# Random-feature attention and a Mish feed-forward on one core: query and key units shifted by one step, and Mish of chunk 0 given priority

## The chip, the cores and the metric

The kernel runs on one core of one Trainium2 chip. The time is device microseconds of one execution; several executions are made and their median is given. A profile shows one more execution, instruction by instruction.

## What is computed

Attention with random features over 8 batches, 8 heads, 576 rows, 64 elements a head and 128 features, and a feed-forward on the result (512 to 2048 to 512), which has Mish between its two products:

```python
def phi(x):
    proj = einsum('bhsd,md->bhsm', x, omega)
    h = proj - sum(x * x, -1) / 2
    h = h - max(h, -1)
    return exp(h) / sqrt(m)
kv  = einsum('bhsm,bhsd->bhmd', phi(k_s), v);  z = sum(phi(k_s), 2)
num = einsum('bhsm,bhmd->bhsd', phi(q_s), kv)
den = einsum('bhsm,bhm->bhs', phi(q_s), z) + 1e-06
x   = (num / den)            # 4608 rows of 512
h   = x @ w_in               # 512 -> 2048
g   = h * tanh(softplus(h))  # Mish
out = g @ w_out              # 2048 -> 512
```

## The kernel before

**Tiles.** Queries come as 36 tiles q0 to q35 of 128 rows with all heads, keys as 4 units per batch (k0_0 is batch 0, heads 0 and 1). The feed-forward goes by chunks of 256 rows: chunk 0 to 3 alone (`ff_in(c)`, `ff_out(c)`), the rest in pairs (`pair_in`, `pair_out`). Most products are made of three fp16 products of high and low parts. At the start, before the weights are split into these parts, the fp32 values are multiplied directly: batches 0 and 1 of the keys (KF = 2), query tiles 0 to 4 (QF = 5) and chunk 0.

**A unit.** `features` (L348) loads a tile, for fp16 units splits it (`in_parts`, L339: a cast on ScalarE and a residual on POOL), projects it on TensorE into PSUM (tiles pk, pq), takes the maximum on VectorE (mxk, mxq) and the exponential on ScalarE (ek, eq). A key unit is then multiplied with the values (pkv, L455 and L490). A query tile below QF goes on in `q_first` (L574): eight transposes on TensorE (pt, L581) with two copies by ScalarE (qp), the product with kv (pn, L592), then on VectorE the denominator (rd, L596) and x (L605), whose copy, residual and transposing DMA into xT are in `x_parts` (L563). Later tiles are transposed by a DMA (L525) and multiplied at L540, with x at L556.

**Weights.** Eight blocks of each matrix come as 64-bit words. `w_task` (L187) assembles fp32 from them (Prelu on ScalarE L198, POOL L201, VectorE L207) and takes the maximum (wmax, L213). `scale_w` makes one scale (s_w) of the eight maxima; `w_split` (L228) then casts a block on ScalarE and makes the residual on VectorE (L82).

**Chunk 0.** `ff_in(0)` (L692) makes 8 PSUM tiles ph, each copied by ScalarE into g with `later(1, cast, ...)`; at the last of them `later(2, mish0)` schedules Mish in place over both halves of g (gr = 1 first, then gr = 0). `ff_out0` (L797) goes over the blocks from f = 15 downward (po, L804).

**The order of the work.** The program is emitted in slots. A slot emits one piece of the feed-forward and then runs `step()`, which goes through an agenda of generators: `yield n` puts the rest of a generator n slots later. `FIRST` (L825) lists the slots at which the units are given in the order k0_0 to k0_3, q0 to q3, k1_0 to k1_3, q4 to q8, k2_0; `GAP` (L840) says how many slots pass between a unit's steps. `FF0` = 17 is the slot at which `ff_in(0)` starts, one ph every two slots; `ff_in(1)` starts at slot 33, `ff_out0` at 49, `ff_in(2)` at 65, alternating with `ff_out(1)`. The compiler then orders each engine's instructions: among those that it reckons ready, the one emitted first goes first. `tc.high_priority(PRIO)` with PRIO = 400 makes an instruction count as emitted 400 instructions earlier. On the chip each engine runs its list strictly in that order.

**PSUM.** ps_h and ps_o have two banks each (ph, po), ps_a four (pk, pq, pt, pn, pkv). A late key unit takes three of ps_a at once, a query tile's pn two.

Of the kernel before, what the change touches and what calls it, by code (L numbers as in the profile page):

```python
# [15 lines left out]
AF = mybir.ActivationFunctionType  # L16
# [14 lines left out]
def tile_kernel(  # L31
# [17 lines left out]
    FT = DF // P  # L49
    CH = 256  # L50
    NCH = NT * P // CH
    FG = 8
    FQ = 4
# [10 lines left out]
    act, dve, pool = nc.scalar, nc.vector, nc.gpsimd  # L64

    def cast(eng, out, in_, scale=1.0):

        if eng is act:
            return act.activation(out, in_, AF.Copy, scale=scale)  # L69
        elif isinstance(scale, float) and scale == 1.0:  # L70
            eng.tensor_copy(out, in_)  # L71
        else:
            eng.tensor_scalar_mul(out, in_, scale)
# [20 lines left out]
    def spin(n, left, right):  # L94
        pi = ps_o.tile([P, 512], F32, tag="o", name=f"spin{nc.next_id()}")
        for _ in range(n):
            nc.tensor.matmul(out=pi[:, 0:right.shape[1]], lhsT=left, rhs=right, start=True, stop=True)  # L97
# [143 lines left out]
    def wi(a, k, f):  # L241
        must(1, "s", 0, f * P * KT // BW)

        o = k * (BW // KT) + f * P % (BW // KT)
        return slots[f * P * KT // BW][:, a, o:o + P]
# [3 lines left out]
    def did(*key):  # L249
        done[key] = done.get(key, 0) + 1  # L250

    def must(n, *key):
        assert done.get(key, 0) >= n, key
# [24 lines left out]
    for i in range(2):  # L278
        t = const.tile([P, 2, 10, D1], F16, name=f"vb{i}")
# [221 lines left out]
    def spans(lo, n):  # L501

        res = []
        for b in range(lo // S, (lo + n - 1) // S + 1):
            res.append((b, max(lo, b * S) - lo, min(lo + n, (b + 1) * S) - lo))
        return res
# [56 lines left out]
    def x_parts(nth, t, x):  # L563
        xs = sb.tile([P, 2, H * D], F16, tag="xs", name=f"xs{t}", bufs=2)
        xf = x.rearrange("p h d -> p (h d)")
        cast(act if nth < 20 else by("x", nth), xs[:, 0], xf)
        rest(by("xlo", nth), xs[:, 1], xf, xs[:, 0])
        yield 1
        nc.sync.dma_start_transpose(
            out=x_at(t), in_=xs.rearrange("p a c -> p (a c)"),  # L570
        )
        did("x", t // 4)

    def q_first(nth, t, e, off):  # L574

        qp = sb.tile([P, H, P], F32, tag="ap", name=f"qp{t}", bufs=2)
        for g in range(2):
            hs = slice(4 * g, 4 * g + 4)
            pt = ps_a.tile([P, 4, P], F32, tag="a", name=f"pt{t}_{g}")
            for i in range(4):  # L580
                nc.tensor.transpose(out=pt[:, i, :], in_=e[:, 4 * g + i, :], identity=ident)  # L581
            cast(act, qp[:, hs, :], pt)
        yield 1
        x = sb.tile([P, H, D], F32, tag="x", name=f"x{t}", bufs=2)
        rd = sb.tile([P, H, 1], F32, tag="rd", name=f"rd{t}")
        for g in range(2):
            hs = slice(4 * g, 4 * g + 4)
            pn = ps_a.tile([P, 4, D1], F32, tag="a", name=f"pn{t}_{g}", padded_shape=[P, 4, P])
            for i in range(4):
                for b, lo, hi in spans(t * P, P):  # L590
                    must(HP, "kvf", b)
                    nc.tensor.matmul(  # L592
                        out=pn[lo:hi, i, :], lhsT=qp[:, 4 * g + i, lo:hi], rhs=kvf[b][:, 4 * g + i, :],
                        start=True, stop=True,
                    )
            dve.tensor_single_scalar(out=rd[:, hs], in_=pn[:, :, D:D1], scalar=EPS, op=ALU.add)  # L596
            dve.reciprocal(out=rd[:, hs], in_=rd[:, hs])
            if t * P < CH:
                xt = dve.tensor_tensor(
                    out=x[:, hs, :], in0=pn[:, :, 0:D], in1=rd[:, hs].broadcast_to([P, 4, D]),  # L600
                    op=ALU.mult,
                )
                continue
            for b, lo, hi in spans(t * P, P):
                xt = dve.scalar_tensor_tensor(  # L605
                    out=x[lo:hi, hs, :], in0=pn[lo:hi, :, 0:D], scalar=vstate[b][2][lo:hi],
                    in1=rd[lo:hi, hs].broadcast_to([hi - lo, 4, D]), op0=ALU.mult, op1=ALU.mult,
                )
        anchors[30 + t] = (xt.ins,)
        if t * P >= CH:  # L610
            yield from x_parts(nth, t, x)
            return
        yield 1
        px = ps_a.tile([P, KT, P], F32, tag="a", name=f"px{t}")
        for i in range(KT):
            nc.tensor.transpose(out=px[:, i, :], in_=x[:, 2 * i:2 * i + 2, :], identity=ident)
        anchors[40 + t] = (cast(act, xT0()[:, :, off:off + P], px).ins, xt.ins)
        if off == 0:
            spin(2, ident, x[:, 0:4, :].rearrange("p h d -> p (h d)"))
        did("x0")  # L620
# [4 lines left out]
    def xT0():  # L625
        return xT[0][:, 0:2 * KT * CH].bitcast(F32).rearrange("p (k s) -> p k s", k=KT)
# [10 lines left out]
    def g0(gr):  # L637
        return gT[0, gr].rearrange("p a f s -> p (a f s)").bitcast(F32).rearrange("p (f s) -> p f s", f=FG)
# [32 lines left out]
    def ff_in(c):  # L671

        must(4 if c > 2 else 2, "x", c // 2) if c else must(2, "x0")
        lo = CH * (c == 3)
        parts = (slice(0, P), slice(P, CH)), (slice(0, CH),)
        sp = [(b_scales(b) if c else None, lo, hi) for b, lo, hi in spans(c * CH, CH)]
        for gr in range(FT // FG):
            gT[c, gr] = sb.tile([P, 2, FG, CH], F16, tag="g", name=f"g{c}_{gr}", bufs=GB)
            for q in range(FG // FQ):
                if c:  # L680
                    h = sb.tile([P, FQ, CH], F32, tag="ht", name=f"h{c}_{gr}_{q}", bufs=HB)
                else:
                    h = g0(gr)[:, q * FQ:(q + 1) * FQ]
                for j in range(0, FQ, 2):
                    ph = ps_h.tile([P, 2, CH], F32, tag="h", name=f"ph{c}_{gr}_{q}_{j}")
                    for part, i in ((part, i) for part in parts[(c, gr, q, j) != (0, 0, 0, 0)] for i in range(2)):
                        f = gr * FG + q * FQ + j + i
                        mm = [(a, y, k) for a, y in ((1, 0), (0, 1), (0, 0)) for k in range(KT)]
                        if c == 0:
                            mm = [(None, None, k) for k in range(KT)]  # L690
                        for n, (a, y, k) in enumerate(mm):
                            ff_mm[0] = nc.tensor.matmul(  # L692
                                out=ph[:, i, part], lhsT=wi(a, k, f) if c else wi0(k, f),
                                rhs=x_two(c // 2)[:, y, k, lo:lo + CH] if c else xT0()[:, k, part],
                                start=n == 0, stop=n == len(mm) - 1,
                            )
                    if c == 0:

                        later(1, cast, act, h[:, j:j + 2, :], ph)
                        if gr == FT // FG - 1 and q == FG // FQ - 1 and j > 0:  # L700
                            later(2, mish0)
                    else:
                        later(1, mish, sp, h[:, j:j + 2, :], ph)
                        if j > 0:
                            later(2, g_split, c, gr, q, sp, h)
                    yield
# [49 lines left out]
    def mish(sp, h, ph):  # L756

        for us, lo, hi in sp:
            anchors["h"] = act.activation(h[:, :, lo:hi], ph[:, :, lo:hi], AF.Mish, scale=us[:, 0:1]).ins  # L759

    def mish0():
        for gr in reversed(range(FT // FG)):
            act.activation(g0(gr), g0(gr), AF.Mish)
            for q in range(FG // FQ):
                did("g", 0, q)

# [55 lines left out]
    GB, HB, QB = 4, 4, 1  # L822
    w_dma = nc.sync

    FIRST = (0, 1, 2, 3, 4, 4, 9, 9, 26, 28, 30, 32, 37, 40, 44, 58, 59, 63)  # L825
    WIS = (6, 7, 8, 9, 11, 12, 13, 14)
    W_MAX = (6, 5, 5, 4, 2, 2, 1, 1)
    WOS = (35, 34, 33, 32, 31, 30, 29, 28)
# [1 line left out]
    W_LOAD, W_LOAD1, W_GAP, PRIO = 1, 2, 1, 400  # L830
# [15 lines left out]
    def gap(what, name):  # L846
        if name in ("k0_0", "k0_1", "k0_2", "k0_3", "q0", "q1"):
            return GAP0[what]
        return GAP[what]

    def pace(c):
# [12 lines left out]
    def start(gen, after=0):  # L864
        agenda.append([slot[0] + after, gen])

    def later(after, fn, *args):
        def gen():
            fn(*args)
            yield 0  # L870
        start(gen(), after)
# [18 lines left out]
    for t in range(NT):  # L890
        last = (t * P + P - 1) // S
# [68 lines left out]
    start(v_task(0))  # L960
    for i, when in enumerate(FIRST):
        at(when, give)
# [94 lines left out]
```

## Time and profile before

| | |
|---|---|
| runs before | 938.16, 938.64, 938.83 us, median 938.64 |
| the profiled execution | 937.79 us, of which the profile's span is 936.0 us |
| granted TensorE clock | 1.00 |
| ScalarE, VectorE, POOL busy | 628.5 us, 529.6 us, 231.1 us |
| bytes moved by DMA | 82.05 MB, mean 88 GB/s |

Engines: PE is TensorE's matmuls, PEld its weight loads, DVE VectorE, ACT ScalarE, POOL GpSimd, SP the engine whose queue issues most DMAs. A row of the timeline has start, length, engine, line, operation, output and inputs with their shapes, and how many instructions it merges; in brackets stands how long the engine was idle before it and on whom it waited. A row of the waits has who waited, for whom, and us in total, times, longest. L69 and L78 to L82 are the helpers `cast` and `rest`, so there the tile's name tells what it is. ACT_TABLE_LOAD is the load of another set of functions into ScalarE.

### The profile page before, as it was taken

How to read it: one execution, taken by the hardware profiler on the slowest of the kernel's cores; microseconds unless marked ns; L12 is line 12 of the kernel's file. 1: busy time of each engine (PE TensorE's matmuls, PEld its weight loads, DVE VectorE, ACT ScalarE, POOL GpSimd, SP SyncE). 2: the span in 40 equal slices, each digit the busy share in tenths (PEclk: the TensorE clock that was granted, in tenths of full speed). 3: DMA queues.
4: the chain of work that ended last, by engine and by line, in shares of the span. 5: the costliest groups of instructions: out<-in, count | busy, mean ns of one | idle time of the engine just before them, and what ended most of it. 6: DMA issues, size and time to landing. Idle time of an engine off the chain costs nothing.

```text
span 936.0 us, 16681 instructions
## 1 busy us (share of the span) xinstructions
PE 921.6 (98%) x6797; PEld 532.4 (57%) x6797; DVE 529.6 (57%) x1019; ACT 628.5 (67%) x914; POOL 231.1 (25%) x143
## 2 busy tenths in 40 slices
PE   9998999999999999999999999999999999999998
PEld 6886866777655555555555555555555555444443
DVE  3899779855646784577357753784476345201200
ACT  5769998996949954897388747963887268304401
POOL 1331143541432233313232232323332121000000
PEclk9999999999999999999999999999999999999999
DMA  9975334623531256214531264203430242101001
GB/s 284 327 210 180 112 70 96 119 86 71 133 94 37 52 122 122 61 28 98 109 89 38 47 128 120 49 24 77 117 50 23 46 113 43 37 1 46 1 1 45
DMA packets 128204, 82.05 MB, mean 88 GB/s; under 512 B 106432, under 2 KB 106560, under 8 KB 128128
## 3 DMA queue, kind: packets, MB, share of 16 engines
q1 hardware_dynamic: 127392, 79.47, 34.1%
q10 hardware_dynamic: 736, 1.52, 0.6%
q8 instruction: 53, 0.87, 0.4%
q14 instruction: 23, 0.19, 0.1%
HBM read 46.37 MB, written 9.44 MB: 60 GB/s over the span
## 4 chain that ended last, share of the span: by engine, by line
PE 89%; DVE 5%; ACT 4%; issue 1%; DMA 0%; POOL 0%; ACTq 0%; DVEq 0%; POOLq 0%
PE po L745 31%; PE ph L721 31%; PE po L787 6%; PE ph L692 5%; PE pq L376 3%; PE pk L376 2%; PE pkv L490 2%; PE pn L540 2%; PE pkv L455 2%; PE po L804 1%; PE spin L97 1%; DVE wmax L213 1%; DVE w L207 1%; PE pk L391 1%; ACT ek L402 1%
## 5 line engine op out<-in xcount | busy, mean ns | idle before, releaser
L721 PE MATMUL ph<-xT,w 128*128 128x512 f16 x1344 | 298.4, 379 | 0.0
L745 PE MATMUL po<-wo,gp 128*128 128x512 f16 x1344 | 296.9, 379 | 0.0
L745 PEld LDWEIGHTS <-gp 128*128 128x128 f16 x1344 | 129.5, 98 | 149.9
L721 PEld LDWEIGHTS <-w 128*128 128x128 f16 x1344 | 129.1, 98 | 148.2
L82 DVE SCALAR_TENSOR_TENSOR gp<-h,us,gp 128x256 f16<-128x256 f32 (+6 forms) x104 | 103.7, 1013 | 121.9 <-ACT gp L69 121.6
L759 ACT ACTIVATE h<-ph,us 128x128 f32<-128x128 f32 (+6 forms) x240 | 108.0, 502 | 46.5 <-PE ph L721 42.4
L78 POOL TENSOR_TENSOR sq<-fq,sq 64x1024 f16<-64x1024 f32 x31 | 67.0, 2163 | 213.9 <-ACT sq L69 118.0
L692 PE MATMUL ph<-xT,w 128*128 128x256 f16 (+2 forms) x720 | 96.4, 290 | 1.3 <-DMA xT<-xs 0.8
L69 ACT ACTIVATE o<-po,us 128x512 f32<-128x512 f32 (+1 forms) x38 | 25.9, 682 | 98.9 <-PE po L745 92.5
L78 POOL TENSOR_TENSOR xs<-x,xs 128x512 f16<-128x512 f32 x34 | 46.0, 1353 | 157.0 <-issue 80.0
L78 POOL TENSOR_TENSOR sk<-fk,sk 64x1152 f16<-64x1152 f32 x24 | 58.3, 2431 | 90.2 <-ACT sk L69 90.1
L397 DVE TENSOR_REDUCE mxk<-pk 128x4 f32<-128x512 f32 (+1 forms) x96 | 49.9, 549 | 45.9 <-PE pk L376 33.4
L69 ACT ACTIVATE gp<-h,us 128x256 f16<-128x256 f32 (+6 forms) x104 | 73.8, 755 | 0.3
L397 DVE TENSOR_REDUCE mxq<-pq 128x4 f32<-128x512 f32 x72 | 46.6, 680 | 43.6 <-PE pq L376 39.5
L787 PE MATMUL po<-wo,g 128*128 128x512 f16 x288 | 65.4, 379 | 0.0
L78 DVE TENSOR_TENSOR qn<-eq,qn 128x1024 f16<-128x1024 f32 x31 | 39.1, 1262 | 43.0 <-ACT qn L69 43.0
L692 PEld LDWEIGHTS <-w 128*128 128x128 f16 x576 | 55.5, 98 | 10.9 <-issue 2.4
L759 ACT ACT_TABLE_LOAD x43 | 55.2, 1283 | 0.8
L69 ACT ACTIVATE sq<-fq 64x1024 f16<-64x1024 f32 x31 | 32.7, 1055 | 31.4 <-issue 29.9
L412 ACT ACT_TABLE_LOAD x39 | 50.0, 1283 | 0.7
L78 DVE TENSOR_TENSOR kp<-ek,kp 128x1152 f16<-128x1152 f32 x24 | 33.9, 1414 | 25.1 <-ACT kp L69 25.1
L78 POOL TENSOR_TENSOR vb<-vf,vb 128x640 f16<-128x640 f32 x24 | 35.9, 1499 | 46.3 <-DVE vb L71 34.5
(127 smaller groups left out, 1063.1 us busy)
## 6 DMA issues: line engine op xcount, KB each, us to landing
vf<-in_vL_dram SPq DMA_DIRECT2D x30, 325.0 KB, 3.2
out_dram<-o SPq DMA_DIRECT2D x36, 256.0 KB, 2.3
fq<-in_qT_dram SPq DMA_DIRECT2D x31, 256.0 KB, 3.4
fk<-in_kT_dram SPq DMA_DIRECT2D x24, 256.0 KB, 3.6
raw<-in_w_out_dram SPq DMA_DIRECT2D x5, 1024.0 KB, 7.1
wo<-in_w_in_dram SPq DMA_DIRECT2D x4, 1024.0 KB, 12.3
raw<-in_w_in_dram SPq DMA_DIRECT2D x4, 1024.0 KB, 14.6
wo<-in_w_out_dram SPq DMA_DIRECT2D x3, 1024.0 KB, 8.3
```

Source lines behind the costliest of these rows:

```text
L69: return act.activation(out, in_, AF.Copy, scale=scale)
L78: ins = eng.tensor_tensor(out=out, in0=in_, in1=hi, op=ALU.subtract)
L82: return eng.scalar_tensor_tensor(out=out, in0=in_, scalar=scale, in1=hi, op0=ALU.mult, op1=ALU.subtract)
L376: nc.tensor.matmul(out=pp[:, i, :], lhsT=left[:, o:o + P], rhs=right, start=j == 0, stop=j == len(terms) - 1,)
L397: sub = dve.tensor_reduce(out=mx[:, lo:hi], in_=pp[:, :m, :], axis=AX.X, op=ALU.max, negate=by_act)
L412: last = act.activation(e, e, AF.Exp, bias=lnt)
L455: nc.tensor.matmul(out=pkv[:, j, :], lhsT=e[:, t, :], rhs=vt[hp][:, u, :], start=i == 0, stop=i == 4,)
L692: ff_mm[0] = nc.tensor.matmul(out=ph[:, i, part], lhsT=wi(a, k, f) if c else wi0(k, f), rhs=x_two(c // 2)[:, y, k, lo:lo + CH] if c else x ...
L721: ff_mm[0] = nc.tensor.matmul(out=ph[:, 0, :], lhsT=wi(a, k, f), rhs=x[:, y, k, :], start=n == 0, stop=n == len(mm) - 1,)
L745: ff_mm[0] = nc.tensor.matmul(out=po[i], lhsT=gP[g, gr][:, a, f % FQ, i * P:(i + 1) * P], rhs=wo(y, f), start=f == 0 and (a, y) == parts[0 ...
L759: anchors["h"] = act.activation(h[:, :, lo:hi], ph[:, :, lo:hi], AF.Mish, scale=us[:, 0:1]).ins
L787: ff_mm[0] = nc.tensor.matmul(out=po[i], lhsT=gT[c, f // FG][:, a, f % FG, i * P:(i + 1) * P], rhs=wo(y, f), start=f == order[0] and (a, y ...
```

## The change

`q_first` gets a `yield 1` ahead of its transposes for t > 1. `FIRST`'s last entry, that of k2_0, goes from 63 to 64. The projection of q6 comes 3 instead of 2 slots behind its residual. The copies of chunk 0's last two ph tiles (gr = 1, q = 1) and all of `mish0` are emitted under `tc.high_priority(PRIO)`, and Mish of gr = 1 is made in two instructions, f = 12 to 15 first.

```diff
     def q_first(nth, t, e, off):
 
+        if t > 1:
+            yield 1
         qp = sb.tile([P, H, P], F32, tag="ap", name=f"qp{t}", bufs=2)
...
-                        later(1, cast, act, h[:, j:j + 2, :], ph)
+                        last = gr == FT // FG - 1 and q == FG // FQ - 1
+                        later(1, urgent if last else cast, act, h[:, j:j + 2, :], ph)
...
+    def urgent(*args):
+        with tc.high_priority(PRIO):
+            cast(*args)
+
     def mish0():
+        with tc.high_priority(PRIO):
+            mish0_()
+
+    def mish0_():
         for gr in reversed(range(FT // FG)):
-            act.activation(g0(gr), g0(gr), AF.Mish)
+            for q in ((1, 0) if gr else (slice(None),)):
+                w = g0(gr)[:, q * FQ:(q + 1) * FQ] if gr else g0(gr)
+                act.activation(w, w, AF.Mish)
             for q in range(FG // FQ):
                 did("g", 0, q)
...
-    FIRST = (0, 1, 2, 3, 4, 4, 9, 9, 26, 28, 30, 32, 37, 40, 44, 58, 59, 63)
+    FIRST = (0, 1, 2, 3, 4, 4, 9, 9, 26, 28, 30, 32, 37, 40, 44, 58, 59, 64)
...
     def gap(what, name):
         if name in ("k0_0", "k0_1", "k0_2", "k0_3", "q0", "q1"):
             return GAP0[what]
+        if what == "lo" and name == "q6":
+            return 3
         return GAP[what]
```

## The prediction

> **What bounds the kernel now.** I read the page's first two lines, the busy time by stages, TensorE's waits, and the chain of waits around the last of these that lies early.
>
> ```profile
> span 936.0 us, 16681 instructions
> PE 921.6 (98%) x6797; PEld 532.4 (57%) x6797; DVE 529.6 (57%) x1019; ACT 628.5 (67%) x914; POOL 231.1 (25%) x143
> ```
>
> TensorE is busy for 921.6 of 936.0 us, so no reordering can win more than the other 14.4 us. The stages (us in the stretch, then busy us of PE, PEld, DVE, ACT, POOL) say where these lie:
>
> ```profile
> 72.00:142.00 70.00, 65.48 (x504) 48.17 (x504) 55.70 (x98) 68.89 (x105) 17.38 (x10) 1.00 0.36 110
> 142.00:180.00 38.00, 35.57 (x316) 24.45 (x315) 32.78 (x73) 32.98 (x38) 16.78 (x9) 1.00 0.55 118
> 180.00:936.00 756.00, 752.12 (x5470) 402.39 (x5468) 388.83 (x735) 481.18 (x666) 176.69 (x99) 1.00 0.29 66
> ```
>
> From 180 us on TensorE idles for 3.88 us, and that is the tail behind its last matmul. All that the change can touch happens before 180 us. There two engines compete to be the bound: in 72 to 142 us ScalarE is busy for 68.89 of 70 us, more than TensorE with 65.48. The waits of TensorE (us in total, times, longest):
>
> ```profile
> PE po L804 <- ACT g L763: 1.8, 1, 1.8
> PE pk L376 <- DVE x L556: 1.6, 1, 1.6
> PE pq L376 <- POOL sq L78: 1.5, 1, 1.5
> PE pt L581 <- ACT eq L402: 1.3, 1, 1.3
> PE pk L391 <- ACT ek L402: 1.1, 1, 1.1
> PE ph L692 <- DMA xT<-xs: 0.8, 1, 0.8
> ```
>
> Four of these stand at places that the diff names: chunk 0's Mish (1.8), q6's projection (1.5), batch 2's keys (1.6), the transposes of q2 (1.3). Together 6.2 us. If each went and nothing took its place, the span would be 929.8 us. The sixth wait is why I don't believe that sum:
>
> ```profile
> 146.08 2.10 POOL xs L78
> 148.20 3.05 DMA xT<-xs
> 151.29 0.81 PE ph L692 x6
> ```
>
> Here TensorE has finished chunk 0's output and q7's projection, and the first matmul of ff_in(2) needs the transposed x of q5, which lands at 151.25. TensorE is 0.8 us early. If it gains 1.8 and 1.5 us before that point, it is 4.1 us early, and the transfer lands when it did. So what is won before 151 us counts only as far as this chain moves too, and the chain comes through the stretch in which ScalarE is full.
>
> **Part by part.** *Mish and the last cast.* ScalarE and, as last row, TensorE (start, us):
>
> ```profile
> 72.72 1.28 ACT L402 ACT_TABLE_LOAD   x1
> 75.90 1.64 ACT L402 ACTIVATE ek<-pk,mxk 128x128 f32<-128x128 f32 x6
> 82.86 0.64 ACT L69 ACTIVATE g<-ph 128x512 f32<-128x512 f32 x1
> 85.58 1.28 ACT L763 ACT_TABLE_LOAD   x1
> 86.88 1.91 ACT L763 ACTIVATE g<-g 128x2048 f32<-128x2048 f32 x1
> 89.85 1.28 ACT L198 ACT_TABLE_LOAD   x1
> 97.10 0.69 ACT L759 ACTIVATE h<-ph,us 128x512 f32<-128x512 f32 x1
> 135.17 1.28 ACT L412 ACT_TABLE_LOAD   x1
> ```
> ```profile
> 70.64 3.72 PE L692 MATMUL ph<-xT,w 128*128 128x256 f32 x16
> ```
>
> The last ph of chunk 0 is ready at 74.4 us and copied at 82.86, 8.5 us later: in program order (slot 32) the copy stands behind the exponentials of k1_0 and k1_1 (slots 30 and 32) and the weight splits. With 400 instructions of priority it and both halves of Mish go ahead of them: 0.64 for the copy, 1.28 for the table, and the halves. One half has 1024 elements a partition: between 0.69 for 512 and 1.91 for 2048 lies 1.10, so two halves are 2.20, 0.29 more than now. A load back to the exponential's table (1.28) follows, but the pair at 85.58 and 89.85 goes, so their number stays. po0 needs f = 15 and 14 first, which lie in the first half. Its 1.80 goes in full, and at least 0.81 of it (1.91 less 1.10) if Mish stayed where it is. What is late next: the exponentials of k1_0 at 75.90 are pushed back by 0.64 + 1.28 + 2.20 + 1.28 = 5.4 us, and TensorE's 1.1 us wait for them (k1_1's projection needs their PSUM banks) can grow by as much. Its cover is ff_in(1)'s first two groups, whose second bank the early copy frees. On the full ScalarE the edit costs 0.29.
>
> By the Trainium skill (ScalarE: Activation LUTs, "What ACT_TABLE_LOAD costs") a switch is 1.28 us and a drain of about 1.38, 2.66 in all, which speaks against putting a Mish between exponentials. Here Mish starts at 86.88, 0.02 us behind its load, so the trace bears out the load and shows no drain.
>
> *q_first one slot later for t > 1* (q2, q3, and q4 as well, which is under QF). q2 and q3 are given at slot 9: their transposes go from slot 14 to 15, pn, x and its copy from 15 to 16, the x DMA on SP from 16 to 17. ff_in(0) starts at slot 17, so its matmuls still rank behind the transposes, and no other PE work is emitted in slots 14 to 16. I therefore leave the 1.3 us at the transposes where they are (ends 0 and 1.3). What does change rank is VectorE: x of q2 and q3 now follows wmax 5, wmax 6 and the assembly (L207) of weight block 7, all slot 16.
>
> ```profile
> 57.17 1.75 DVE L207 SCALAR_TENSOR_TENSOR w<-raw,w 128x1024 int32<-128x1024 int32 x1
> 58.84 0.81 DVE L301 TENSOR_REDUCE vmx<-vf 128x1 f32<-128x640 f32 x1
> 59.57 1.20 DVE L213 TENSOR_REDUCE wmax<-w 128x1 f32<-128x1024 f32 x1
> 68.21 1.15 ACT L69 ACTIVATE w<-w,s_w 128x1024 f16<-128x1024 f32 x1 [1.78 <-DVE s_w L133]
> ```
>
> The row at 59.57 is the last maximum before the scale s_w, on which every weight split waits (ScalarE idled 1.78 for it). The same work precedes it either way, but x can now fill the place of the vmx at 58.84: s_w comes 0.7 us earlier (ends 0 and 1.8). That moves the whole ScalarE chain. x itself is wanted only by ff_in(1), which follows chunk 0's last ph (74.4 us), so its delay of a few us is covered; without that cover it would cost its own length.
>
> q4: transposes from slot 42 to 43, pn, x and its copy from 43 to 44, the x DMA from 44 to 45, past ff_in(1)'s sixth group (emitted at slot 43).
>
> ```profile
> 116.94 1.09 ACT L69 ACTIVATE qp<-pt 128x512 f32<-128x512 f32 x2 [0.25 <-PE pt L581]
> 119.92 1.04 ACT L69 ACTIVATE sq<-fq 64x1024 f16<-64x1024 f32 x1
> ```
>
> The two copies of q4 (1.09, and 0.25 of idle for them) stand ahead of q5's cast at 119.92, where q5's chain to 151 us begins. Going behind it, they free 1.3 us (ends 0 and 1.3). q4's own x DMA ran long before q5's; SP loses nothing by one place.
>
> *q6's projection one slot later* (50 to 51): chunk 0's block 6 output at slot 51 has run by then, so its place on TensorE hardly changes; its wait is POOL's:
>
> ```profile
> 121.10 2.13 POOL L78 TENSOR_TENSOR sq<-fq,sq 64x1024 f16<-64x1024 f32 x1 [12.97 <-issue]
> 124.24 2.27 POOL L78 TENSOR_TENSOR xs<-x,xs 128x512 f16<-128x512 f32 x1 [1.01 <-ACT xs L69]
> 126.59 5.19 POOL L78 TENSOR_TENSOR sq<-fq,sq 64x1024 f16<-64x1024 f32 x2
> 124.58 1.04 ACT L69 ACTIVATE sq<-fq 64x1024 f16<-64x1024 f32 x1
> ```
>
> q4's residual (124.24, now later) stood in front of q6's at 126.59. Without it q6's starts when its cast ends, 125.6, and takes 2.2: 0.9 of the 1.5 us goes (ends 0 and 1.5). q6's later steps, its two transposing DMAs among them, follow by a slot; its x is for ff_in(3).
>
> *Sum before 151 us:* TensorE gains 1.8 + 0.9 = 2.7, the x chain 0.7 + 1.3 - 0.3 = 1.7. The smaller counts: **1.7 us**, and the wait for xT grows from 0.8 to 1.8.
>
> *k2_0 one slot later* (given at 64). Its two loads on SP go with it, and keep their three slots ahead of the cast. Its projection moves from slot 69 to 70, behind an output group, while k2_1's stays at 71.
>
> ```profile
> 165.87 0.89 DVE L397 TENSOR_REDUCE mxk<-pk 128x4 f32<-128x512 f32 x2 [3.69 <-PE pk L376]
> 166.68 0.68 DVE L406 TENSOR_TENSOR ek<-pk,mxk 128x512 f32<-128x512 f32 x1
> 171.90 1.73 DVE L71 CAST vb<-vf 128x640 f16<-128x640 f32 x2
> ```
>
> k2_1's third bank waits for x of q7 on VectorE, behind the vb casts of k2_0. These go from slot 71 to 72, behind q7's x: 1.7 us leave. But the first two rows (1.5 us), now behind 3.69 us of idle, come into the crowd instead. Net 0.2, or 1.6 if all goes, or a longer wait by 1.5, since k2_0, q7 and k2_1 want 3 + 2 + 3 of four banks closer together; I take **0.4**, near the row arithmetic.
>
> Total 1.7 + 0.4 = 2.1 us: span 933.9, the profiled execution 937.79 becomes 935.7. The median of the runs lies 0.85 above it: 938.64 - 2.1 = 936.5.
>
> **The rivals.** B, *all of it comes off*: the chain moves by as much as TensorE gains, q2's wait goes, k2's too. 6.2 us gives 932.4, two thirds of it 934.5. For it: four named waits; against: the full ScalarE and the unchanged rank of q2.
>
> C, *taken back at 151 us*: the x chain does not move, the wait for xT becomes 3.5 us, and only k2 counts: 938.2 (938.6 without). For it: ScalarE has 1.1 us idle in 70, so its order, not its load, would have to do it.
>
> D, *slower through table loads*: Mish cuts the exponentials of k1 in such a way that a pair of loads is added. There are 13 from the one at 72.72 to the one at 135.17; a fourteenth and fifteenth put 2.57 us into the full ScalarE, and q5's x, with ff_in(2), comes 2.6 us later: 941.2, or 940.8 with k2. It decides from the first added pair on, as there is only 1.1 us of idle to swallow it; TensorE's own 5.4 us at k1 points the same way, for it has only the 4.5 us of its idle time there to give. With the drain of the skill's page the pair would be 5.3, 944.
>
> E, *the clock*: in C TensorE idles 3.5 us in one piece at 151, twice the longest wait of this trace (1.8), through which the granted clock stayed at 1.00. If it sank to half for the 2.6 us group behind it, C's 938.2 becomes 940.8. The Trainium skill (TensorE: Matmul & The Clock Gate, "The HAM clock gate") has it fall to 4/8 after about 3.4 us of idling; no run here shows such a gap.
>
> **The numbers.** About 0.2%, 1.9 us, is what can be told from no change. Forecast A (936.5; own range 935.2 to 937.8) 0.42, of it 0.28 below 936.8 and 0.14 within; B 0.17; C 0.21; D 0.15; E 0.05. Faster 0.45, same 0.35, slower 0.20. The range from 933.2 to 940.6 leaves out part of B and most of D and E.
>
> **What would show it.** Right: no wait of po for Mish; Mish before 82 us in two rows at 1.1; the last cast near 75; 13 table loads; s_w before 68; q2's wait still there; the wait for xT at 1.5 to 2 us and ff_in(2) starting near 149.6; k2's wait at about 1.2. Wrong: ff_in(2) at 151 or later (C, D), a wait of over 4 us for ek, q2's wait gone (B), or any idle time of TensorE after 180 us.

## The result and the profile after

The change makes the kernel slower: 950.97 us (median of 4 runs, 949.53 to 953.32) against 938.57 (median of 4) for the kernel before, a ratio of 1.0135 with a 95% interval of 1.0123 to 1.0147. The profiled execution took 950.43 us. In two experiments below (e7 and e16) the profiled execution fell into a state with a low clock throughout, so no time is read from those two profiles.

The page's first lines, and TensorE's waits (us in total, times, longest):

```profile
span 948.6 us, 16684 instructions
PE 930.2 (98%) x6797; PEld 535.1 (56%) x6797; DVE 534.5 (56%) x1019; ACT 624.8 (66%) x911; POOL 227.5 (24%) x143
```
```profile
PE pn L540 <- DMA qp<-qn: 3.6, 1, 3.6
PE pk L376 <- DVE ek L406: 2.4, 1, 2.4
PE pk L391 <- ACT ek L402: 2.2, 2, 1.6
...
PE pt L583 <- ACT eq L402: 1.3, 1, 1.3
```

The span grew by 12.6 us. Idle time of TensorE is 948.6 - 930.2 = 18.4 us, 4.0 more than the 14.4 before. The other 8.6 us are busy time, of the same 6797 matmuls. The stages, in the columns of the prediction's (the last but two is the granted clock), show where the matmuls grew longer:

```profile
72.00:142.00 70.00, 67.20 (x481) 48.19 (x480) 55.02 (x95) 62.88 (x100) 14.24 (x9) 0.98 0.36 113
142.00:180.00 38.00, 33.22 (x259) 21.82 (x257) 27.74 (x59) 27.95 (x33) 11.12 (x5) 0.91 0.46 99
180.00:200.00 20.00, 16.79 (x155) 11.31 (x154) 18.22 (x34) 15.63 (x20) 10.54 (x7) 0.83 0.43 102
200.00:948.60 748.60, 744.71 (x5402) 396.61 (x5398) 383.39 (x724) 472.19 (x654) 172.19 (x96) 1.00 0.29 66
```

Before, the clock was 1.00 throughout. Now it falls in three places; narrower windows put bounds on them:

```profile
87.40:90.80 3.40, 3.40 (x5) 1.04 (x4) 3.06 (x4) 3.40 (x10) 0.00 (x0) 0.52 0.77 232
...
145.30:152.10 6.80, 5.42 (x29) 3.14 (x30) 5.99 (x11) 3.33 (x4) 0.40 (x1) 0.50 0.60 125
...
182.90:189.70 6.80, 5.47 (x20) 2.38 (x21) 6.08 (x15) 4.86 (x6) 4.05 (x4) 0.50 0.46 138
```

Length times (1 - clock) is 3.4 x 0.48 + 6.8 x 0.50 + 6.8 x 0.50 = 8.4 us. I call it lost clock time below. It counts the whole length of a dip, though TensorE was busy for only 5.42 and 5.47 us of the last two. Over its busy time it is 3.4 x 0.48 + 5.42 x 0.50 + 5.47 x 0.50 = 7.1 us. So the clock explains 7.1 of the 8.6 us of added busy time; the other 1.5 us are not traced to a cause. In the other 748.6 us the clock is 1.00, and the idle time is the old 3.9 us of the tail.

So there are two things to explain: new waits of TensorE (4.0 us net), and a clock that halves behind them (7.1 us). The waits stand near 81 to 85, 143 to 147 and 181 to 184 us.

**At 81 to 85: exponentials of k1.** ScalarE, then TensorE:

```profile
66.74 1.06 ACT L776 ACTIVATE g<-g 128x1024 f32<-128x1024 f32 x1
...
74.97 0.89 ACT L402 ACTIVATE ek<-pk,mxk 128x128 f32<-128x128 f32 x3
...
77.34 0.36 ACT L402 ACTIVATE ek<-pk,mxk 128x128 f32<-128x128 f32 x1
77.72 1.28 ACT L776 ACT_TABLE_LOAD   x1
79.02 1.06 ACT L776 ACTIVATE g<-g 128x1024 f32<-128x1024 f32 x1
...
81.13 1.28 ACT L402 ACT_TABLE_LOAD   x1
82.43 0.37 ACT L402 ACTIVATE ek<-pk,mxk 128x128 f32<-128x128 f32 x1
```
```profile
80.24 1.02 PE L817 MATMUL po<-wo,g 128*128 128x512 f32 x2
82.85 1.16 PE L391 MATMUL pk<-om_f,fk 64*128 64x128 f32 x14 [1.58 <-ACT ek L402]
84.66 0.44 PE L391 MATMUL pk<-om_f,fk 64*64 64x128 f32 x4 [0.66 <-ACT ek L402]
```

Mish now ends at 80.1 and po0 begins at 80.24 without a wait. One half of it already ran at 66.74, since its own columns were copied by then. The other half, with a table load on each side, stands in the middle of k1_0's nine exponentials: 4.7 us lie between the fourth (77.7) and the fifth (82.4).

**At 143 to 147: x of q4, then q5.** VectorE, then TensorE:

```profile
124.67 0.16 DVE L598 TENSOR_SCALAR rd<-pn 128x4 f32<-128x4 f32 x1 [3.38 <-PE pn L594]
...
127.04 2.07 DVE L82 SCALAR_TENSOR_TENSOR kv<-kvf,kv 128x8 f16<-128x8 f32 x1
...
130.21 0.97 DVE L607 SCALAR_TENSOR_TENSOR x<-pn,s_v,rd 64x256 f32<-64x256 f32 x2
131.21 1.29 DVE L397 TENSOR_REDUCE mxq<-pq 128x4 f32<-128x512 f32 x2
```
```profile
121.88 1.04 PE L583 MATMUL pt<-ident,eq 128*128 128x128 f32 x8
...
146.68 1.50 PE L540 MATMUL pn<-kv,qp 128*128 128x65 f16 x24 [3.61 <-DMA qp<-qn]
...
158.78 1.47 PE L694 MATMUL ph<-xT,w 128*128 128x256 f16 x12 [0.34 <-DMA xT<-xs]
```

q4's transposes (121.88, before at 116.30) now stand behind ff_in(1)'s sixth group too, and its x reaches VectorE 4 us later (the first rd at 124.67, before at 120.62). q5's maxima stand behind q4's x on VectorE in both kernels, and so they go from 125.53 to 131.21. All of q5's chain shifts with them: its matmul with kv starts at 146.68 (139.17 before), and ff_in(2) at 158.78, 7.5 us later than before.

**At 181 to 184: the keys of batch 2.** TensorE, then VectorE:

```profile
183.99 0.40 PE L376 MATMUL pk<-om,sk 128*128 128x128 f16 x2 [2.44 <-DVE ek L406]
```
```profile
181.21 2.13 DVE L71 CAST vb<-vf 128x640 f16<-128x640 f32 x1
```

The projection of k2_1 waits for a subtraction on VectorE (183.26), which stands behind a cast of the values. That one cast took 2.13 us, where two of them took 1.73 in the kernel before (171.90). No run was made for this place alone; k2_0's step by itself (e4 below) leaves no wait like it.

### The profile page after: what moved, and what is told of

The parts are those of the page before. It is cut to its first block, busy times and chain, and to the rows that moved or that the text cites. A ratio compares the mean times of both kernels' runs of the same rounds, so it can differ in the third digit from the quotient of the medians.

```text
span 948.6 us, 16684 instructions
## 1 busy us (share of the span) xinstructions
PE 930.2 (98%) x6797; PEld 535.1 (56%) x6797; DVE 534.5 (56%) x1019; ACT 624.8 (66%) x911; POOL 227.5 (24%) x143
## 4 chain that ended last, share of the span: by engine, by line
PE 89%; DVE 5%; ACT 2%; DMA 2%; issue 1%; POOL 0%; ACTq 0%; SPq 0%; POOLq 0%
PE po L748 31%; PE ph L724 30%; PE po L800 6%; PE ph L694 5%; PE pq L376 3%; PE pn L540 3%; PE pk L376 2%; PE pkv L490 2%; PE po L817 2%; PE pkv L455 2%; DMA qp<-qn 1%; PE pn L594 1%; PE pk L391 1%; DMA fk<-in_kT_dram 1%; DVE wo L82 1%
## 5 line engine op out<-in xcount | busy, mean ns | idle before, releaser
L800 PE MATMUL po<-wo,g 128*128 128x512 f16 x288 | 67.9, 388 | 0.0
L69 ACT ACTIVATE xs<-x 128x512 f16<-128x512 f32 x34 | 21.3, 627 | 45.2 <-DVE x L556 34.2
```

Of the source, the lines that this page charges most:

```text
L800: ff_mm[0] = nc.tensor.matmul(out=po[i], lhsT=gT[c, f // FG][:, a, f % FG, i * P:(i + 1) * P], rhs=wo(y, f), start=f == order[0] and (a, y ...
```

## The experiments

P is my working theory: the parts that put work of one unit past the queues of other engines do the harm, and each such delay costs twice, as a wait and as clock. Spans and busy times are compared with before's 936.0 and 921.6 us.

**e1: the steps of q2, q3 and q4 alone.**

```diff
     def q_first(nth, t, e, off):
+        if t > 1:
+            yield 1
```

> The kernel before with the yield in q_first alone (q2, q3, q4). Theory Q (q4's later steps put its x on VectorE ahead of q5's maximum, so that ff_in(2) starts late and the clock falls in the wait): most of the 12.4 us are here, 944 to 948 us, ff_in(2) at 156 or later, a clock of 0.5 near 145. Theory M (Mish between the exponentials of k1 starves TensorE, the clock falls, and all that follows is late): this part alone costs little, 937 to 940 us, and the clock stays at 1.00.

942.65 us, ratio 1.0044 (1.0029 to 1.0059). The one large new wait is 2.6 us for ek of k1_0, and behind it stands one stretch of half clock from 80.5 to 83.9 (1.7 us lost). ff_in(2) starts at 153.94. So neither theory holds as it stood: theory Q wanted 156 or later and most of the loss here, theory M a clock of 1.00.

**e2: the Mish part alone** (early last copy, Mish with priority, second half in two).

```diff
-                        later(1, cast, act, h[:, j:j + 2, :], ph)
+                        last = gr == FT // FG - 1 and q == FG // FQ - 1
+                        later(1, urgent if last else cast, act, h[:, j:j + 2, :], ph)
...
+    def mish0():
+        with tc.high_priority(PRIO):
+            mish0_()
```

> The kernel before with the Mish part alone (early copy, priority, two halves). Theory M: waits of TensorE for ek of 2 us or more near 82 us, a clock of 0.5 for some 3.4 us behind them, and most of the loss, 944 to 948 us. Theory Q: the same stall near 82 us but no late ff_in(2); at most the 2 us of that stall and its clock, 938 to 941 us.

945.31 us, 1.0066 (1.0048 to 1.0083). TensorE's waits for ek are only 0.77 and 0.66 us, 0.3 more than before, so the cover that I had named for the idle time holds. But the clock halves all the same. The first stretch below holds both short waits, the second lies behind it:

```profile
82.00:85.40 3.40, 1.97 (x22) 1.51 (x22) 1.97 (x3) 3.39 (x8) 0.00 (x0) 1.00 0.00 0
85.40:92.30 6.90, 6.90 (x23) 4.68 (x22) 6.57 (x8) 6.90 (x15) 0.00 (x0) 0.51 0.48 134
```

With a further dip at 181 us, 5.1 us of clock time are lost, and 8.3 us of span.

**e3 and e4: q6's projection alone, k2_0 alone.**

```diff
+        if what == "lo" and name == "q6":
+            return 3
```
```diff
-    FIRST = (..., 44, 58, 59, 63)
+    FIRST = (..., 44, 58, 59, 64)
```

> The kernel before with q6's projection one slot later, alone. Theories M and Q both: within 1 us of before, 937.6 to 939.6, since its place on TensorE hardly changes. A theory that q6 makes the late x of q5 would want 941 or more.

> The kernel before with k2_0 one slot later, alone. Theory K (the crowding on ps_a is this part's own): TensorE waits 2 us or more near 175, the clock falls there, 940 to 943 us. If the wait of 2.4 us after the change is a consequence of the late ff_in(2) instead: 937 to 939 us and the 1.6 us wait at most as long as it was.

937.95 us, 0.9996 (0.9986 to 1.0006), and 937.93 us, 0.9993 (0.9983 to 1.0002): no difference that can be told from none, no dip. q6's wait stayed whole, k2's fell from 1.6 to 0.6, and 0.2 for a second bank. The rows of the waits, of e3 and then of e4:

```profile
PE pq L376 <- POOL sq L78: 1.5, 1, 1.5
```
```profile
PE pk L376 <- DVE x L556: 0.6, 1, 0.6
```

**e5 and e6: the steps of q2 and q3, and that of q4, apart** (`if t in (2, 3)`, `if t == 4`).

> The kernel before with the yield for q2 and q3 alone. Theory P (x of q2 and q3, now later on VectorE, makes their residuals on POOL late; these hold up the assembly of w_out's blocks, which stands on VectorE ahead of the second weight split and of k1_0's maximum, so the exponentials of k1_0 come late and TensorE waits 2.6 us for them, after which the clock falls): all of e1's 4 us are here, 941 to 944 us, the wait for ek at 2.4 us or more and a clock near 0.5 at 81 to 84 us. Rival (the loss of e1 is q4's): 938 to 939.5 us, the wait for ek at 1.1.

> The kernel before with the yield for q4 alone. Theory P: within 1 us of before (937.5 to 939.5), the clock at 1.00 throughout. Rival (q4's late x holds up q5 on VectorE by itself): 941 or more, ff_in(2) at 153 us or later.

942.54 us, 1.0040 (1.0025 to 1.0055), and 942.12 us, 1.0040 (1.0029 to 1.0052). I had forecast q4 harmless; that fell. Its wait is the 3.6 us of the changed kernel at nearly the same place, with 1.7 us of clock lost behind it:

```profile
144.34 0.92 PE L540 MATMUL pn<-kv,qp 128*128 128x65 f16 x24 [3.61 <-DMA qp<-qn]
```

In e5 the wait is 2.3 us for ek, and the clock is at half from 81.1 to 91.3 us, with 5.1 us lost. The two losses, 3.9 and 3.5 us, do not add up to e1's 4.2.

Nor is the loss the clock's alone. Each execution has its own mean clock: e6's fastest had 1.000 and took 941.59 us, 2.9 more than before's median. In e5 the profiled execution (942.39 us) had 0.995, and three others with 0.998 took 942.02 to 943.38. So where the chain of x is late by itself, clock time lost ahead of it seems to come partly in place of a wait; that is an inference, as only one execution of each was traced.

**e7: e1, with TensorE kept at work in the wait for ek** (ten idle matmuls).

```diff
+                            if (c, gr, q, j, i, n) == (1, 0, 0, 0, 1, 3):
+                                with tc.issue_after(ff_mm[0].ins), tc.high_priority(PRIO):
+                                    spin(10, ident, ident)
```

> e1 with ten idle matmuls (some 2 us) put on TensorE into the wait for ek, so that the wait stays but TensorE isn't idle in it; their result is used by nothing. Theory C (the wait itself is harmless, since the x chain sets ff_in(2); what costs is the clock at half speed behind it): the clock stays at 1.00 and the time falls by 2 us or more against e1, to 939 to 940.5. Rival (the wait costs by itself): no gain against e1, 942 to 943.5, though the clock stays at 1.00.

943.8 us, 1.0050 (1.0033 to 1.0067), no faster than e1. With no usable profile it can't be said whether the clock stayed up there, so e7 settles nothing.

**e8 and e10: the wait by itself.** Waits of TensorE of chosen lengths in the last pair's output, where nothing else hangs on it. ScalarE makes them with a chain of copies, of which n, one number for each place, sets the length. Lines left out below choose the places and hold the next product back until the wait is over.

```diff
+    def wait(n):
+        ...
+        with tc.issue_after(ff_mm[0].ins):
+            nc.tensor.matmul(out=pi[:, 0:P], lhsT=ident, rhs=ident, start=True, stop=True)
+        ...
+        act.activation(t[:, 0:P], pi[:, 0:P], AF.Copy)
+        for _ in range(n):
+            act.activation(t, t, AF.Copy)
+        ...
+        gate[0] = nc.tensor.matmul(out=pj[:, 0:P], lhsT=ident, rhs=t[:, 0:P], start=True, stop=True).ins
```

> The kernel before with five waits of growing length put into the last pair_out, 10 us apart, where nothing else runs: a matmul, then 2, 3, 4, 5 and 7 copies on ScalarE, then a matmul that needs their result, and the output's matmuls behind it; some 1.5, 2.1, 2.6, 3.2 and 4.3 us. Theory C: behind the longer ones the granted clock is at 0.5 for some us and the 12 matmuls that follow take up to twice 2.6 us; behind 1.5 us it stays at 1.00. Rival (only waits early in the kernel, with other engines full, lower it): 1.00 behind all five, and the span grows by the waits alone, 14 to 16 us.

In e8 only two of the five places existed in this loop: one wait was 1.38 us (no dip), the other stood at the very end. e10 has seven.

> The kernel before with seven waits of TensorE put into the last pair's output (five tiles' matmuls apart or so), made by a chain of copies on ScalarE: about 2.1, 2.8, 2.1, 2.8, 3.5, 3.5 and 5.0 us long. Nothing else is changed. Theory C (a wait of more than about 2.2 us makes the granted clock sink to one half for about 3.4 us behind it): the clock stays at 1.00 behind those of 2.1 and shows dips to 0.5 behind the other five, some 1.7 clock-us lost for each, 8.5 in all. Rival (the clock falls by the length in proportion, or only from 3.4 us of idling on): dips behind the last three alone, 5.1 clock-us. Rival (the dips of the changed kernel come from something else than the waits): none here. The span is the former 936.0 plus 21.8 of waits plus the lost clock-us and some 3 us for the extra matmuls.

971.84 us, one execution. First the first four waits, then windows of the same kernel: the first row holds the first wait itself, each of the others lies behind one of the four.

```profile
899.66 0.49 PE L750 MATMUL wait<-wt,ident 128*128 128x128 f32 x2 [2.04 <-ACT wt L748]
...
907.96 0.53 PE L750 MATMUL wait<-wt,ident 128*128 128x128 f32 x2 [2.41 <-ACT wt L748]
...
917.22 0.49 PE L750 MATMUL wait<-wt,ident 128*128 128x128 f32 x2 [1.69 <-ACT wt L748]
...
925.46 0.80 PE L750 MATMUL wait<-wt,ident 128*128 128x128 f32 x2 [2.35 <-ACT wt L748]
```
```profile
896.50:899.90 3.40, 1.36 (x9) 0.82 (x7) 0.00 (x0) 1.54 (x3) 0.00 (x0) 1.00 0.01 2
900.00:903.40 3.40, 3.40 (x18) 1.55 (x16) 0.48 (x1) 0.00 (x0) 0.00 (x0) 1.00 0.00 0
908.00:911.70 3.70, 3.70 (x11) 1.49 (x12) 0.48 (x1) 0.00 (x0) 0.00 (x0) 0.54 0.00 0
917.50:921.00 3.50, 3.50 (x18) 1.60 (x18) 0.48 (x1) 0.00 (x0) 0.00 (x0) 1.00 0.00 0
925.30:928.80 3.50, 3.34 (x9) 1.59 (x10) 0.48 (x1) 0.11 (x1) 0.00 (x0) 0.51 0.00 0
```

Behind the waits of 2.04 and 1.69 us the clock stays at 1.00 and a window holds 18 matmuls; behind 2.41 and 2.35 it is at half for about 3.4 us and holds 11 and 9. The waits of 3.01 (twice) and 4.69 us had such dips too, the last one twice as long. Theory C holds: a wait alone, with no other change, costs clock. A limit at 3.4 us of idle would have left only the last dip.

**e9 and e11: which parts are harmless.** e9 is the kernel before with Mish's second half in two (no priority), q6's step and k2_0's. e11 is the whole Mish part but the priority of `mish0` itself.

> The kernel before with only those parts of the change that reorder nothing ahead of q5's x chain: Mish's second half in two (without the priority), q6's projection one slot later, k2_0 one slot later. Theory P (the harm is in what is moved past VectorE's, GpSimd's and ScalarE's queues, the steps of q2 to q4 and the priority; the parts left here are harmless): po0's wait for Mish falls from 1.8 to about 1.0, k2's from 1.6 to about 0.8, no dip of the clock, 937.2 us, ratio 0.9975 to 0.9995. Rival: what is won before 151 us comes back as a longer wait for xT of q5, so only k2's counts: 938.0, ratio 0.9990 to 1.0005. Rival: any of these parts feeds the same clock dips, then 940 or more.

> The Mish part without Mish's own priority: the last copy of chunk 0 goes first, Mish's second half goes in two, but Mish stays at its place behind the exponentials of k1. Nothing else is changed. Theory P (in the Mish part it is Mish with its two table loads between k1_0's maxima and its exponentials that pushes the eks back and q5's chain with them): no wait for ek beyond the 1.1 of before, no dip, po0's wait about 1.0 or less, 937.5 to 938.5. Rival (the early copy alone lets ff_in(1)'s first groups in too early and moves the weight splits, and that does the harm): waits for ek or for x of over 2 us, dips, 942 or more.

e9: 937.15 us, 0.9987 (0.9978 to 0.9996). e11: 937.47 us, 0.9987 (0.9978 to 0.9997). No dip in either. e11 differs from e2 by the priority of Mish alone, and by 7.8 us. Its remaining half stays behind the exponentials, with the pair of loads where it was:

```profile
86.44 1.28 ACT L770 ACT_TABLE_LOAD   x1
87.73 1.06 ACT L770 ACTIVATE g<-g 128x1024 f32<-128x1024 f32 x1
89.84 1.28 ACT L198 ACT_TABLE_LOAD   x1
```

**e12: the change without its Mish part.**

> All of the change but its Mish part: the steps of q2, q3 and q4 one slot later, q6's projection and k2_0 one slot later. Theory P (the parts add up up to the clock dips): steps alone gave 942.65, q6 and k2 alone -0.5 each, so 941.7, ratio 1.0025 to 1.0045, with the dip near 80 us of the steps alone. Rival (the parts feed one another also without Mish): 944 or more, a second dip near 145 us behind the wait for qp of q5.

943.54 us, 1.0048 (1.0034 to 1.0062): 4.9 us, about the steps' own loss. One dip, 85.6 to 92.5 us, 3.4 us lost.

**e13: q2's and q3's steps without GpSimd's order.** In e5 the residuals of q2 and q3 run 4 to 6 us later on GpSimd, and by the program's own rule the conversions (L201) of the first w_out blocks wait behind them. In e13 they don't.

```diff
+        lo_ = anchors.get("lo", ())
         rest(by("xlo", nth), xs[:, 1], xf, xs[:, 0])
+        if t in (2, 3):
+            anchors["lo"] = lo_
```

> The steps of q2 and q3 one slot later, alone, but their residuals on GpSimd no longer hold back the conversions (L201) of the first two w_out blocks, which then run ahead of them as data allows. Theory P (the loss of 4.0 us of these steps comes through GpSimd: VectorE's L207 waits 2.04 us in order for the delayed L201, s_w comes at 68.8 instead of 68.0, k1_0's maxima at 74.6 instead of 72.2, and the eks after them): no wait of VectorE for L201, s_w at 67 or before, the wait for ek back to about 1, no dip, 937.5 to 939. Rival (the loss comes from x and the second weight split on VectorE, or from ScalarE's order, and GpSimd only follows): s_w moves, but the wait for ek stays over 2 us with its dip, 941.5 or more.

941.74 us, 1.0036 (1.0022 to 1.0050). The theory fell. VectorE's scale is early and its wait for L201 gone, but k1_0's maxima now stand behind a second weight split (at 72.41) and come 1.5 us later than before. VectorE:

```profile
67.23 0.15 DVE L133 TENSOR_SCALAR s_w<-s_w 128x1 f32<-128x1 f32 x1
...
73.68 0.68 DVE L397 TENSOR_REDUCE mxk<-pk 128x4 f32<-128x512 f32 x1
```

Of its 3.8 us of span, 3.5 are busy time: two waits for ek (1.50 and 1.18 us) and half clock from 84.6 to 91.4.

**e14: q4's step five slots later**, so that its x falls behind q5's maxima.

```diff
+        if t == 4:
+            yield 5
```

> The step of q4 alone, but five slots later in place of one, so that q4's x falls behind the maxima and exponentials' subtractions of q5 on VectorE. Theory P (the loss of 3.5 us of q4's step comes from x of q4, delayed on TensorE to 122.3 us and now crowding q5's maxima, which go from 125.5 to 128.9): q5's maxima come at 125 or before, no wait for qp of q5 over 1 us near 140, no dip there, 937.5 to 939.0. Rival (whatever delays q4 delays ff_in(2), as its own transposed x comes last): a wait for xT of 2 to 4 us near 150 that now names q4's transfer, 940.5 to 943.

938.74 us, 1.0004 (0.9994 to 1.0013). As expected at this place. There is one dip elsewhere, from 174.8 to 178.2 us, behind waits of only 0.90, 0.53 and 0.53 us around k2's projection. q5's maxima (VectorE) and ff_in(2) (TensorE) are earlier than in the kernel before (125.53, 151.29):

```profile
123.73 1.27 DVE L397 TENSOR_REDUCE mxq<-pq 128x4 f32<-128x512 f32 x2
```
```profile
150.88 1.37 PE L694 MATMUL ph<-xT,w 128*128 128x256 f16 x11
```

**e15 to e18: what is left.** e15 has the harmless parts together (early copy, split, q6, k2_0). e16 is e13 with priority for the maxima of k1_0 and k1_1, e17 that priority alone, e18 is e15 with it.

```diff
-            sub = dve.tensor_reduce(
+            with tc.high_priority(PRIO) if name in ("k1_0", "k1_1") else ExitStack():
+                sub = dve.tensor_reduce(
```

> The change without its steps of q2, q3 and q4 and without Mish's own priority: the early last copy, the second half in two, q6's projection and k2_0 one slot later. Theory P (these reorder nothing ahead of q5's chain, and each keeps its small gain): no dip, po0's wait near 1, k2's near 0.5, 937.0, ratio 0.9970 to 0.9995, at least as fast as the same without the early copy (937.15). Rival (the early copy and k2's step together make a new wait): 938.5 or more.

> As e13 (the steps of q2 and q3 one slot later, conversions of w_out not held back), and the maxima of k1_0 and k1_1 on VectorE get 400 instructions of priority, so that k1_0's run ahead of the second weight split again. Theory V (the loss of 3.3 us comes from the place of k1_0's maxima: they went from 72.2 to 73.7 us and the table load and exponentials behind them from 72.7 to 74.9): maxima near 72, the load near 73, no wait for ek over 1.2, no dip, 937.5 to 939. Rival (ScalarE's own order of weight splits and exponentials, or x of q2 and q3 behind them, does it): maxima early, but the waits for ek or qp and the dip stay, 941 or more.

> The control: the kernel before with the priority for the maxima of k1_0 and k1_1, and nothing else. In the kernel before k1_0's maxima stand ahead of the second weight split already, so theory V expects no change but for k1_1's: 938 to 939, ratio 0.9990 to 1.0010. Rival (the priority moves something else that matters): outside of that.

> The harmless parts of the change (early last copy, second half in two, q6's projection and k2_0 one slot later) and the priority for the maxima of k1_0 and k1_1. If the exponentials of k1 are what is late next, 936.5 or less; if they are not, 937.3 as without the priority; if the weight splits that the maxima pass are later missed, 938.5 or more.

e15: 937.31 us, 0.9987 (0.9979 to 0.9996). e16: 941.81, 1.0031 (1.0020 to 1.0042). e17: 939.81, 1.0030 (1.0004 to 1.0056). e18: 936.34, 0.9977 (0.9968 to 0.9985), the fastest of all and ahead of both kernels. Theory V, that the maxima's place is the cause for q2 and q3, is not borne out: e16 is as slow as e13, though in its list on VectorE k1_0's maxima do stand ahead of the second weight split. e17 missed what I expected (938 to 939): alone the priority costs 1.3 us, while on top of e15 it gains 1.0, and why is not shown. So what exactly in q2's and q3's step delays k1's exponentials stays open; GpSimd's order and the maxima's place are each not enough. That the loss is mostly clock behind those waits holds for the traced executions of e5 and e13.

## Why the prediction was wrong

- *Mish and the last cast.* Right: po0's wait is gone, Mish runs in two rows of 1.06 before 82 us, no table load is added (12 from 60.34 to 140 us where the kernel before has 14 from 59.54), Mish starts 0.02 us behind its load (77.72 + 1.28, 79.02). The last cast came at 76.87, 1.9 later than I said, as a weight split and three exponentials stood ahead of it. The step that failed is "On the full ScalarE the edit costs 0.29": Mish's priority costs 7.8 us (e2 less e11), on ScalarE's order and not its load. I had counted the exponentials' delay and named ff_in(1) as their cover. That covers the idle time (1.4 us in e2 for 1.1), not the sparse stretch in which the clock falls, and not the units behind k1.
- *q2 and q3.* Right: the transposes' 1.3 us stay. Wrong: "s_w comes 0.7 us earlier". On VectorE x did move behind the maxima, but I had not followed x's residual to GpSimd, where L201 waits behind it. GpSimd, then VectorE, of the changed kernel:

```profile
64.15 1.16 POOL L78 TENSOR_TENSOR xs<-x,xs 128x512 f16<-128x512 f32 x1 [2.58 <-ACT xs L69]
65.39 3.35 POOL L201 TENSOR_SCALAR wo<-wo 128x1024 int32<-128x1024 uint8 x2
```
```profile
66.53 1.23 DVE L207 SCALAR_TENSOR_TENSOR wo<-wo 128x1024 int32<-128x1024 int32 x1 [2.04 <-POOL wo L201]
...
68.59 0.15 DVE L133 TENSOR_SCALAR s_w<-s_w 128x1 f32<-128x1 f32 x1
```

  VectorE waits 2.04 us there, in order, and s_w comes at 68.59 instead of 68.04. With that taken away (e13) s_w did come 0.8 us earlier, at 67.23: the arithmetic was right, and worth nothing, for the time stayed at 941.7. The term was -0.7 (part of the sum); measured +3.9 (e5).
- *q4.* Wrong in sign: "they free 1.3 us" for q5's cast. The cast did go ahead of q4's copies (at 121.45, since all was later by then), but q5's next step, its maxima, stands behind q4's x on VectorE, and that x now came 4 us later. I had called its delay harmless by looking only at SP's queue. Measured +3.5 us alone (e6); e14, which moves x past the maxima, takes it back.
- *q6.* "0.9 of the 1.5 us goes": nothing went in e3. But the term rested on a later residual of q4, and e3 doesn't move that. With q4's step the wait is 0.56 us in e6 and in the changed kernel, there for x on VectorE, and still 1.5 us in e1 and e12, so it hangs on what else has moved. *k2_0.* "0.4": 0.8 of the wait went (e4). In the changed kernel the wait grew to 2.44 us instead: the first cast of k2_0's values did not go behind q7's x (181.21, x at 185.43).
- *Sum before 151 us.* "The smaller counts" took the x chain for a gain of 1.7; it lost 7.5, and ff_in(2) began at 158.78 instead of the 149.6 forecast. Of my signs for wrong, two showed in the trace: ff_in(2) behind 151, and idle time after 180 us.
- *The clock (rival E, 0.05).* The row (3.61 us of wait) came out as C had it, 3.5, but at q5's product with kv, 8 us ahead of where I put it, and E's price was too small: I let the clock fall once, for a group of 2.6 us, where it fell three times, for 3.4, 6.8 and 6.8 us, 7.1 us of them lost in busy time. I also used the longest undisturbed wait of the trace (1.8 us) as a comfort, when a wait of 2.35 us can be enough for a fall (e10), only half a us more. By the Trainium skill (TensorE: Matmul & The Clock Gate, "The HAM clock gate") a free-running window of about 3.4 us is watched. The dips' lengths of 3.4 us and its double agree, and so do their starts: in the changed kernel 87.27, 145.30 and 182.85 us, which are 17 and 11 times 3.41 us apart. A wait as long as the window isn't needed here.
- *Why the range missed.* Its upper end, 940.6, lay below even D (941.2) and E (940.8), which have one cause each. But three parts each put ff_in(2) at 155.6 to 155.9 us when made alone (e2, e5, e6), 4.3 to 4.6 later than before, and each has a wait over 2 us or a sparse stretch that takes 1.7 to 5.1 us of clock.

The sum of the single parts (e2 6.8, e5 3.9, e6 3.5, e3 and e4 -0.5 each) is 13.2; the change costs 12.4. With e1 in place of e5 and e6 the sum is 10.0, so the nearness of the first sum proves nothing: the parts are not independent.

## What to carry to other kernels

Before moving a step, follow everything it emits to every engine's in-order list, and ask there who now stands behind it: for q4 the harm came from its x on VectorE, not from the transposes that were meant (for q2 and q3 the place stays open). A kernel that is 98% busy at full clock has more to lose than its idle time, since a wait of about 2 us can be paid again in clock. And a priority on work whose own wait is 1.8 us should not cut into a chain (here the exponentials of the keys) on which later units hang; the split and the early copy alone left 1.3 of the 1.8 us of that wait, and still gained 1.2 us (e11).

## What the runs showed of the hardware

- The granted clock of TensorE fell to 0.50 behind each idle wait of 2.35 us or more in e10, and not behind its waits of 2.04 and 1.69 us, with wide fp16 products around. In e10 the dip begins 2.2 to 2.7 us after the wait's start, in e1 and e5 3.9 and 4.0 us after it. The lost clock time of the traces comes in steps of 1.7 us: 1.7 in e1 and e6, 3.4 in e12 and e13, 5.1 in e2 and e5.
- The length of a wait does not decide alone. e5 and e12 have the same wait of TensorE for ek:

```profile
79.38 1.52 PE L391 MATMUL pk<-om_f,fk 64*128 64x128 f32 x18 [2.30 <-ACT ek L402]
```
```profile
79.69 1.52 PE L391 MATMUL pk<-om_f,fk 64*128 64x128 f32 x18 [2.31 <-ACT ek L402]
```

  In e5 the clock fell at 81.1 us; in e12 it stayed at 1.00 until 85.65, behind a later wait of 1.16 us. In the same way a wait of 2.20 us for q7's x has a fall behind it in e2 (181.1) and none in e17. In each trace that has dips the clock changes only at multiples of 3.41 us from one another. In e12 an edge of this grid (78.82) cuts the wait (77.38 to 79.69) in two. That what counts is the work within one stretch of the grid fits these four runs, but it is an inference: no run moved the grid.
- It can fall with shorter waits too: behind 0.77 and 0.66 us in e2, and behind 0.90, 0.53 and 0.53 us in e14. What TensorE does in the rest of the stretch seems to matter. In e2 the stretch of the grid from 82.13 to 85.55 has 2.02 of 3.41 us busy, mostly in half-high (64x128) fp32 products, and the clock fell behind it; that from 153.81 to 157.23 has only 1.45 us busy, in 128x256 fp16 products, and the clock stayed at 1.00.
  That the clock follows the work in the array and not the busy share is an inference from these two; no run was made for it.
- A small operation of VectorE can take eleven times its time: the kv row of 128x8 took 0.19 us in the kernel before and 2.07 us at 127.04 in the changed one, where GpSimd ran q6's residual from 126.94 to 129.06 and both end together. It is 1.9 of the 5.7 us by which q5's maxima are late. That GpSimd holds VectorE up there is only inferred from the times; no run was made for it.
